# Two-layer attention and GLU kernel: second layer from its unit 3 on written in orders of four steps, with 16, 7 and 2 buffers of three kinds

## The chip, the cores and the metric

One core of a Trainium2 chip runs the whole program. The metric is the time of one execution on the device, in microseconds (us). Each kernel is run several times and the median is taken.

## The reference, cut to what matters

The same two sublayers run twice over 2048 rows of 448 numbers, in float32: attention with 16 query heads of 28 that share one key and one value head, then a gated unit of width 1792.

```python
def _A_ref(x, wq, wk, wv, wo):
    q = (x @ wq).reshape(B, S, H, Dh).transpose(0, 2, 1, 3)
    k = x @ wk
    v = x @ wv
    p = _softmax(jnp.einsum("bhqd,bkd->bhqk", q, k) * (Dh ** -0.5), axis=-1)
    o = jnp.einsum("bhqk,bkd->bhqd", p, v)
    return o.transpose(0, 2, 1, 3).reshape(B, S, H * Dh) @ wo

def _B_ref(x, w_gate, w_up, w_down):
    return (_sigmoid(x @ w_gate) * (x @ w_up)) @ w_down

x = A_x
x = x + _A_ref(_layernorm(x), wq, wk, wv, wo)
x = x + _B_ref(_layernorm(x), w_gate, w_up, w_down)
# and both once more, with the same weights
```

## The kernel before, in words

The 2048 rows are cut into 16 units of 128 query rows (`U`), the keys into 16 tiles of 128 (`KT`). A layer is a loop over 16 x 16 steps: in step `kt` of unit `u` the program makes the scores of the unit's 16 heads against one key tile. All instructions stand in the order in which the program writes them; each engine works through its own in that order.

Four kinds of work make up a step, and one letter stands for each in the strings of `PATHS`:

- **S** (`scores`, L580 to 588): one matmul of four heads (tile `s`, L584, 96 rows of keys by 512 columns), and on ScalarE the exponential of it into a tile `P` (L587). A step has four.
- **P** (`pv`, L590): the values. The four `P` tiles of one earlier step are multiplied with `VV`, each by a float32 matmul that uses 32 columns of the array (L595, at column positions 0, 32, 64 and 96), and summed over the unit's steps in one PSUM tile `pv`. In the trace each of these matmuls is two records, so one step's values are eight. Steps whose values are still to be made stand in the list `waiting`.
- **M** (`Maxima.step`): the row maxima of a later unit, which the scores need as an offset. Four matmuls `mx` use 32 rows of the array each (L549, at row positions 0, 32, 64 and 96) and fill four PSUM tiles; VectorE reduces each (L554, tile `mp`).
- **F** (`fill.slice`): a slice of everything else on the TensorE. The feed-forward of a block of two units (`TB` = 2) runs here: seven passes of `glu` with 44 matmuls for the gate (`gp`) and for the up projection (`up`, both L352), then the down projection (`dn`, L784), and the output projection of the attention (`wo`, L695). Each F gives out as many nanoseconds of it as `rate` says, so that what is left is spread over the steps that are left; 28 us of it (`KEEP`) stay for the end.

**X** issues the next stage of the chain that follows a unit's values (sums, division, output projection, layer norm) and has no time of its own on the TensorE.

A pair of strings describes two successive steps: the first one's order and the second's. "A" and "B0"/"B1" are the first layer's, "C" the second layer's units 0 to 2. From unit 3 on the second layer takes "D0" for even and "D1" for odd units. There the values of two steps are made together in the first of two steps, behind its four scores.

All PSUM tiles but `pv` share seven banks (`NBK`). A bank that was given back longest ago is taken next, so an S or an M waits until the exponential, the reduction or the GLU's activation that reads that bank's last contents is done. In SBUF, `P` has 12 buffers, the GLU's products `h` have 10 (`HB`), and the tag `s2` has three: it holds `th`, the gate's tanh (L746), which VectorE multiplies with `up` (L754) and from which the two halves of `h` are made (L757 on ScalarE, L758 on VectorE). At the start of the program the 16 tiles of the input take ten buffers of `h` and six of `P` (`load_x0`), and `s2` holds scratch of the scales (`junq`) and copies of query projections (`qf`, L409).

Of the kernel before, what the change touches and what calls it, by code (L numbers as in the profile page):

```python
# [8 lines left out]
F32 = mybir.dt.float32  # L9
# [10 lines left out]
def interleaved_layers_kernel(ctx: ExitStack, tc: tile.TileContext, x, wq, wk, wv, wo, wg, wu, wd, out, layers=2):  # L20
# [7 lines left out]
    _, S, D = x.shape  # L28
    F = wg.shape[1]
    H, Dh = 16, 28  # L30
    NT, NB, G, KT, FC = S // 128, S // 512, H // 4, S // 128, F // 128
    U = NT
    TB, WB, HB = 2, 4, 10
    NBL = NT // TB
    EPS = 1e-5

# [5 lines left out]
    wk1 = ctx.enter_context(tc.tile_pool(name="wk1", bufs=2))  # L42
# [37 lines left out]
    def fps(shape, dt, name):  # L80
        flush()
        return psf.tile(shape, dt, tag="f", name=name, bufs=NBK["f"])
# [262 lines left out]
    def chain(ps, W, X, cost, w_first):  # L345

        pairs = PAIRS if w_first else sorted(PAIRS, key=lambda a: a[2])
        for n, (part, c, xc, k) in enumerate(pairs):
            a, b = W(part, c, k), X(xc, k)
            if not w_first:  # L350
                a, b = b, a
            nc.tensor.matmul(ps, a, b, start=n == 0, stop=n == 10)  # L352
            yield cost
# [43 lines left out]
    def qproj(l, XT, b, g):  # L397
        p = fps([128, 512], F32, "qp")
        yield from chain(p, lambda a, c, k: WQ[:k, a, c, 4 * g:4 * g + 4].rearrange("p h d -> p (h d)"),
                         lambda c, k: XT[:k, c], C512, True)  # L400
        by_pool = early[0] or (l, b) == (1, 1)

        def ev():
            q = wk1.tile([128, 2, 512], F16, name="qst")
            hi = QH0[:, g] if l + b == 0 else q[:, 0]
            nc.scalar.activation(hi, p, AF.Copy, scale=2.0 ** -18)
            if by_pool:
                f = wk1.tile([128, 512], F32, tag="s2", name="qf", bufs=3)
                nc.scalar.activation(f, p, AF.Copy, scale=2.0 ** -18)  # L409

            def lo():
                QDONE[l, b] = QDONE.get((l, b), 0) + 1
                if by_pool:
                    nc.gpsimd.tensor_tensor(q[:, 1], f, hi, op=OP.subtract)
                else:
                    nc.vector.scalar_tensor_tensor(q[:, 1], p, 2.0 ** -18, hi, op0=OP.mult, op1=OP.subtract)
                if l + b == 0:
                    nc.sync.dma_start(qd[0][0, g, 0], hi)
                    nc.sync.dma_start(qd[0][0, g, 1], q[:, 1])
                else:  # L420
                    nc.gpsimd.dma_start(qd[l % 2][b, g].rearrange("l p n -> p l n"), q)
            defer(lo)
        defer(ev)
# [157 lines left out]
    def scores(l, u, kt, g, P):  # L581
        assert ("m", l, u) in stored, (l, u, kt)
        s = psf.tile([128, 512], F32, tag=BANKS["s"], name="s", bufs=NBK[BANKS["s"]])
        nc.tensor.matmul(s, KK[l][0:96, 0, kt * 128:(kt + 1) * 128], QS[l, u][:, g].rearrange("p h n -> p (h n)"),  # L584
                         start=True, stop=True)
        p = wk1.tile([128, 512], F32, tag="P", name="P", bufs=12)
        nc.scalar.activation(p, s, AF.Exp, scale=esc)  # L587
        P.append(p)

# [32 lines left out]
    class Block:  # L622
# [109 lines left out]
        def bulk(self):  # L732
            l, b, XT2 = self.l, self.b, self.XT2
            hs = []

            def glu(f):

                for j in range(2):
                    if f + j + 2 < FC:
                        self.load_w(f + j + 2)  # L740
                w = [self.wt.pop(f + j) for j in range(2)]
                gp = fps([128, 2, TB * 128], F32, "gp")
                for j in range(2):
                    yield from chain(gp[:, j], lambda a, c, k: w[j][:k, 0, a, c], lambda c, k: XT2[:k, c], C256, True)
                th = wk1.tile([128, 512], F32, tag="s2", name="th", bufs=3)
                defer(lambda: nc.scalar.activation(th, gp.rearrange("p j n -> p (j n)"), AF.Tanh, scale=gsc))  # L746
                up = fps([128, 2, TB * 128], F32, "up")
                for j in range(2):
                    yield from chain(up[:, j], lambda a, c, k: w[j][:k, 1, a, c], lambda c, k: XT2[:k, c], C256, True)
                h = wk1.tile([128, 2, 512], F16, name="h", bufs=HB)  # L750

                def ev():
                    t = th
                    nc.vector.scalar_tensor_tensor(t, th, 1.0, up.rearrange("p j n -> p (j n)"), op0=OP.add, op1=OP.mult)  # L754

                    def parts():
                        nc.scalar.activation(h[:, 0], t, AF.Copy, scale=2.0 ** -17)  # L757
                        defer(lambda: nc.vector.scalar_tensor_tensor(h[:, 1], t, 2.0 ** -17, h[:, 0], op0=OP.mult,  # L758
                                                                     op1=OP.subtract), 3)
                    defer(parts, 3)  # L760
                defer(ev)
                hs.append(h)

            for f in range(0, FC, 2):
                yield from glu(f)

            if not self.last and b % 2 == 0:
                XTQ[l + 1, b // 2] = big.tile([128, 7, 512], F16, tag="big", name="XT1")
            need(2 + FC)
            for t in range(TB):  # L770
                yield from self.down(t, hs)
# [113 lines left out]
    fill = Filler()  # L885
# [7 lines left out]
    xr0 = {}  # L893

    def load_x0(i, eng=nc.sync):
        if i < HB:
            xr0[i] = wk1.tile([128, D], F32, tag="h", name="xr0", bufs=HB)
        else:
            xr0[i] = wk1.tile([128, D], F32, tag="P", name="xr0", bufs=12)
        eng.dma_start(xr0[i], x[0, i * 128:(i + 1) * 128])  # L900

    hl0, ls0 = {}, {}
# [77 lines left out]
    nmx = 0  # L980

    def qsq(c):
        junk = wk1.tile([128, D], F32, tag="s2", name="junq", bufs=3)
        squares(parts[:, c:c + 1], rq[:, c], junk)

    def qsum():
# [45 lines left out]
    for b in range(1, NB):  # L1032
# [5 lines left out]
    HEAD = U * KT - 32  # L1038
    sparse = ()
    PATHS = {  # L1040
        "A": ("FFSFSSFSPXM", "FSFSFSSPXM"),
        "B0": ("FSFSSXSPPM", "SFFSSFFXMFS"),
        "B1": ("FSFSFXSFSPMP", "SSFSFFXSFM"),
        "C": ("FFSXSSSPPM", "SFFXFFSMSSF"),
        "D0": ("FFXFSSSSPPM", "FFSFSXSFFMS"),
        "D1": ("FSFXSFSSPPM", "SSFFFXSFSFM"),
    }

    def pair_of(l, u):
# [9 lines left out]
    for l in range(layers):  # L1059
# [20 lines left out]
        rate = 0.0  # L1080
        for step in range(U * KT):
            u, kt = divmod(step, KT)
            if step == HEAD and not final:
                mxs[l + 1] = Maxima(l + 1)
            P = []
            pair = pair_of(l, u)
            single = "P" in pair[0] and "P" in pair[1]
            for o in pair[kt % 2]:
                if o == "S":
                    scores(l, u, kt, len(P), P)  # L1090
                elif o == "M":
                    if l and step < 3 * KT:
                        n = step in sparse
                    else:
                        n = 1 + (u == 0 and kt in MORE)
                    if not n:
                        mx.visit()
                    for _ in range(n):
                        if not mx.step() and not final and l + 1 in mxs:
                            a = mxs[l + 1].between()  # L1100
                            if a and soon(a[0], mxs[l + 1].need(a)):
                                mxs[l + 1].step(a)
                    if kt == 2 and u + 1 < U:
                        load_qs(l, u + 1)
                elif o == "P":
                    for _ in range(len(waiting) if single else min(1, len(waiting))):
                        pv(*waiting.pop(0))
                elif o == "X":
                    if u and kt == 1:
                        b = (u - 1) // TB  # L1110
                        if (l, b) not in BLK:
                            BLK[l, b] = Block(l, b)
                        later(*BLK[l, b].tile(u - 1))
                    if l == 0:
                        paced(step)
                    tick()
                    fed = sum(BLK[l, b].fed == TB for b in range(NBL) if (l, b) in BLK)
                    if fed < NBL - 1:
                        rate = fill.left / max(FIRST + TB * KT * fed - step, 1)
                    else:  # L1120
                        rate = max(fill.left - KEEP, 0) / (U * KT - step)
                else:
                    fill.slice(2 * rate / "".join(pair).count("F"))
            waiting.append((l, u, kt, P))
        while waiting:
            pv(*waiting.pop(0))
# [46 lines left out]
```

## Time and profile before

| what | us |
|---|---|
| median of 3 runs | 2245.24 (2240.86 to 2248.77) |
| the profiled execution's own time | 2247.71 |
| span of the instructions in it | 2245.9 |
| second layer, unit 3's first score to unit 15's last (13 units) | 1350.5 to 2158.3: about 808 |
| an odd unit and the next even unit there | 62.6 and 63.35 |
| last score to end of the span | about 88 |

The profiled execution lies 2.5 us above the median of the runs, of which 1.8 us lie around the span. The shares of the span by engine are PE 98%, VectorE (DVE) 73%, ScalarE (ACT) 69%. In the timeline, start times on PE are recorded; how long a matmul took is modelled and includes its way through the array, so the distance from one start to the next is what a matmul costs in a stream.

### The profile page before, as it was taken

How to read it: one execution, taken by the hardware profiler on the slowest of the kernel's cores; microseconds unless marked ns; L12 is line 12 of the kernel's file. 1: busy time of each engine (PE TensorE's matmuls, PEld its weight loads, DVE VectorE, ACT ScalarE, POOL GpSimd, SP SyncE). 2: the span in 40 equal slices, each digit the busy share in tenths (PEclk: the TensorE clock that was granted, in tenths of full speed). 3: DMA queues.
4: the chain of work that ended last, by engine and by line, in shares of the span. 5: the costliest groups of instructions: out<-in, count | busy, mean ns of one | idle time of the engine just before them, and what ended most of it. 6: DMA issues, size and time to landing. Idle time of an engine off the chain costs nothing.

```text
span 2245.9 us, 41454 instructions
## 1 busy us (share of the span) xinstructions
PE 2195.5 (98%) x15915; PEld 1030.8 (46%) x15915; DVE 1643.7 (73%) x2905; ACT 1552.8 (69%) x2595; POOL 335.9 (15%) x590
## 2 busy tenths in 40 slices
PE   7998999999999999999999999999999999999999
PEld 3322344444544445454564324445454544445467
DVE  7888888777777787777796557777777777777222
ACT  5698777776667677676614997777676767777741
POOL 5113764101010100101012010000000000000010
PEclk9999999999999999999999999999999999999999
DMA  4333662323313232331441113323231313223233
GB/s 143 106 97 94 197 215 81 106 79 85 112 60 102 64 100 90 97 107 49 119 154 35 36 52 108 80 88 99 67 108 49 100 59 103 76 88 96 75 118 108
DMA packets 203622, 213.28 MB, mean 95 GB/s; under 512 B 135376, under 2 KB 164240, under 8 KB 203424
## 3 DMA queue, kind: packets, MB, share of 16 engines
q1 hardware_dynamic: 198080, 195.78, 29.2%
q0 software_dynamic: 5344, 14.87, 1.9%
q8 instruction: 124, 2.03, 0.4%
q14 instruction: 74, 0.61, 0.1%
HBM read 175.37 MB, written 23.59 MB: 89 GB/s over the span
## 4 chain that ended last, share of the span: by engine, by line
PE 86%; DVE 8%; ACT 2%; issue 1%; DMA 1%; SPq 1%; POOL 0%; DVEq 0%; ACTq 0%; POOLq 0%
PE pv L595 20%; PE s L584 19%; PE up L352 11%; PE dn L784 11%; PE gp L352 11%; PE mx L549 7%; DVE mp L554 6%; PE wo L695 3%; PE qp L352 2%; ACT P L587 1%; DMA wgu<-wgu_d 0%; DMA rq<-in_A_wq_dram 0%; DMA rc<-sums 0%; PE hot L916 0%; DVE sgu L131 0%
## 5 line engine op out<-in xcount | busy, mean ns | idle before, releaser
L587 ACT ACTIVATE P<-s,esc 128x512 f32<-128x512 f32 x2048 | 1297.8, 690 | 474.5 <-PE s L584 462.8
L554 DVE TENSOR_REDUCE mp<-mx 128x1 f32<-128x512 f32 x2048 | 1269.4, 682 | 389.2 <-PE mx L549 385.4
L584 PE MATMUL s<-QS,KK 96*128 96x512 f16 x2048 | 673.8, 381 | 21.3 <-DVE mp L554 14.8
L352 PEld LDWEIGHTS <-wgu 128*128 128x128 f16 x4928 | 467.6, 97 | 182.1 <-issue 42.9
L595 PE MATMUL pv<-P,VV 128*32 128x512 f32 x4096 | 510.7, 602 | 0.0
L352 PE MATMUL gp<-XT,wgu 128*128 128x256 f16 x2464 | 349.2, 272 | 2.4 <-DVE mp L554 1.7
L352 PE MATMUL up<-XT,wgu 128*128 128x256 f16 x2464 | 348.3, 272 | 0.7 <-DVE mp L554 0.7
L784 PE MATMUL dn<-WD,h 128*128 128x448 f16 x1344 | 301.0, 352 | 0.0
L584 PEld LDWEIGHTS <-KK 96*128 96x128 f16 x2048 | 189.7, 97 | 212.5 <-issue 114.5
L595 PEld LDWEIGHTS pv<-P,VV 128*32 128x32 f32 x4096 | 98.7, 108 | 244.6 <-issue 242.6
L549 PE MATMUL mx<-KK,QH 32*128 32x512 f16 x1792 | 185.3, 386 | 3.0 <-DVE mp L554 1.7
L784 PEld LDWEIGHTS <-h 128*128 128x128 f16 x1344 | 126.5, 97 | 129.4 <-issue 14.5
L549 PEld LDWEIGHTS <-QH 32*128 32x128 f16 x1792 | 46.0, 91 | 256.5 <-issue 252.7
L669 POOL TENSOR_TENSOR lb<-pvs,lb 128x512 f32<-128x512 f32 x32 | 41.1, 1284 | 739.1 <-DMA lb<-sums 619.8
L757 ACT ACTIVATE h<-th 128x512 f16<-128x512 f32 x112 | 70.3, 628 | 61.8 <-DVE th L754 61.5
L754 DVE SCALAR_TENSOR_TENSOR th<-th,up 128x512 f32<-128x512 f32 x112 | 76.2, 680 | 48.9 <-PE up L352 42.2
L306 POOL TENSOR_SCALAR rs<-mv 128x1 f32<-128x1 f32 (+1 forms) x50 | 11.2, 225 | 656.6 <-DVE mv L291 573.6
L352 PE MATMUL qp<-XT,WQ 128*128 128x512 f16 x352 | 108.3, 390 | 0.7 <-DVE mp L554 0.4
L746 ACT ACTIVATE th<-gp,gsc 128x512 f32<-128x512 f32 x112 | 76.8, 685 | 32.8 <-PE gp L352 32.6
L758 DVE SCALAR_TENSOR_TENSOR h<-th,h 128x512 f16<-128x512 f32 x112 | 79.9, 713 | 20.8 <-ACT h L757 20.8
L695 PE MATMUL wo<-WO,oT 128*128 128x448 f16 x384 | 89.7, 352 | 0.2 <-ACT P L587 0.2
L352 PEld LDWEIGHTS <-WQ 128*128 128x128 f16 x352 | 32.9, 99 | 54.9 <-issue 28.9
(151 smaller groups left out, 918.1 us busy)
## 6 DMA issues: line engine op xcount, KB each, us to landing
wgu<-wgu_d SPq DMA_DIRECT2D x224, 512.0 KB
QS<-qd SPq DMA_DIRECT2D x384, 32.0 KB
lb<-sums SPq DMA_DIRECT2D x128, 64.0 KB
xr<-in_A_x_dram SPq DMA_DIRECT2D x32, 224.0 KB
qd<-qst POOLq DMA_DIRECT2D x28, 256.0 KB, 2.7
wgu_d<-sgu POOLq DMA_DIRECT2D x14, 512.0 KB, 3.7
x2d<-x SPq DMA_DIRECT2D x16, 224.0 KB
xr<-x2d SPq DMA_DIRECT2D x16, 224.0 KB
```

The costliest lines, as they stand in the source:

```text
L352: nc.tensor.matmul(ps, a, b, start=n == 0, stop=n == 10)
L549: nc.tensor.matmul(ps[h][:, i * w:(i + 1) * w], qh[32 * h:32 * h + 32, g], KK[l][32 * h:32 * h + 32, 1, ka:kz], start=True, stop=True, til ...
L554: nc.vector.tensor_reduce(o, ps[h].rearrange("p (g k) -> p g k", g=n), axis=AX.X, op=OP.max)
L584: nc.tensor.matmul(s, KK[l][0:96, 0, kt * 128:(kt + 1) * 128], QS[l, u][:, g].rearrange("p h n -> p (h n)"), start=True, stop=True)
L587: nc.scalar.activation(p, s, AF.Exp, scale=esc)
L595: nc.tensor.matmul(v[32 * g:32 * g + 32], VV[l][:, kt], P[g], start=kt == 0, stop=kt == KT - 1, tile_position=(0, 32 * g))
L695: nc.tensor.matmul(p, v["oT"][:, a, h * 128:(h + 1) * 128], WO[:, c, h], start=n == 0, stop=n == 11)
L746: defer(lambda: nc.scalar.activation(th, gp.rearrange("p j n -> p (j n)"), AF.Tanh, scale=gsc))
L754: nc.vector.scalar_tensor_tensor(t, th, 1.0, up.rearrange("p j n -> p (j n)"), op0=OP.add, op1=OP.mult)
L757: nc.scalar.activation(h[:, 0], t, AF.Copy, scale=2.0 ** -17)
L758: defer(lambda: nc.vector.scalar_tensor_tensor(h[:, 1], t, 2.0 ** -17, h[:, 0], op0=OP.mult, op1=OP.subtract), 3)
L784: nc.tensor.matmul(p, hs[f // 2][:, a, o:o + 128], WD[:, f, c], start=n == 0, stop=n == 3 * FC - 1)
```

## The change

The strings of "D0" and "D1" become four each: the order is now written for four steps, and which string a step takes is `kt % 4`. The letters of four steps are the same in number (16 S, 4 M, 4 X, 4 P; D1 has 15 F in place of 16, and each gives out correspondingly more). The values (P) stand at the end of the first step and in the second: one step's at the end of the first, the others before and after the maxima of the second. In the third and the fourth step there are none. Since up to 16 probability tiles now wait for their values, `P` has 16 buffers; `h` has 7 and `s2` has 2. At the start the input therefore takes seven buffers of `h` and nine of `P`.

```diff
-    TB, WB, HB = 2, 4, 10
+    TB, WB, HB = 2, 4, 7
...
-                f = wk1.tile([128, 512], F32, tag="s2", name="qf", bufs=3)
+                f = wk1.tile([128, 512], F32, tag="s2", name="qf", bufs=2)
...
-        p = wk1.tile([128, 512], F32, tag="P", name="P", bufs=12)
+        p = wk1.tile([128, 512], F32, tag="P", name="P", bufs=16)
...
-                th = wk1.tile([128, 512], F32, tag="s2", name="th", bufs=3)
+                th = wk1.tile([128, 512], F32, tag="s2", name="th", bufs=2)
...
-        "D0": ("FFXFSSSSPPM", "FFSFSXSFFMS"),
-        "D1": ("FSFXSFSSPPM", "SSFFFXSFSFM"),
+        "D0": ('FFXFSSSSP', 'MPPFSXSPMFFFSS', 'XSFFFSFSMFSFF', 'SSXFSFMS'),
+        "D1": ('FFXFSSSSP', 'PMPSFFXSPMFSFS', 'FSFSSFXMFSF', 'SFSFSFXMS'),
...
-            single = "P" in pair[0] and "P" in pair[1]
-            for o in pair[kt % 2]:
+            single = len(pair) == 2 and "P" in pair[0] and "P" in pair[1]
+            for o in pair[kt % len(pair)]:
...
-                    fill.slice(2 * rate / "".join(pair).count("F"))
+                    fill.slice(len(pair) * rate / "".join(pair).count("F"))
```

The tiles `xr0` and `junq` take the same new numbers of buffers. "A" to "C" keep their orders.

On PE, in an even unit (unit 8 of the second layer, first step of a group of four): before, the last score is followed by the values of two steps and the maxima. The names are `s` score, `pv` values, `mx` maxima's product, with `KK` the keys, `QH` the queries' high halves and `VV` the values.

```order
L584 MATMUL s<-QS,KK 128x512
L595 MATMUL pv<-P,VV 32x512 x8
L549 LDWEIGHTS QH
L549 MATMUL mx<-KK,QH 128x512
L549 LDWEIGHTS QH
L549 MATMUL mx<-KK,QH 128x512
L549 LDWEIGHTS QH
L549 MATMUL mx<-KK,QH 128x512
L549 LDWEIGHTS QH
L549 MATMUL mx<-KK,QH 128x512
L352 LDWEIGHTS wgu
```

After the change the same place on PE reads so:

```order
L584 MATMUL s<-QS,KK 128x512
L595 MATMUL pv<-P,VV 32x512 x4
L549 LDWEIGHTS QH
L549 MATMUL mx<-KK,QH 128x512
L549 LDWEIGHTS QH
L549 MATMUL mx<-KK,QH 128x512
L549 LDWEIGHTS QH
L549 MATMUL mx<-KK,QH 128x512
L549 LDWEIGHTS QH
L549 MATMUL mx<-KK,QH 128x512
L595 MATMUL pv<-P,VV 32x512 x8
L352 LDWEIGHTS wgu
```

The run of eight has become a run of four, the maxima, and a run of eight; a third run, of four, follows further down in the same step, where before the next run was two steps away. In the whole stretch from unit 3's first score to the end, PE's order has 105 uninterrupted runs of values before and 152 after, and 188 groups of maxima in both.

On VectorE, a stretch around units 7 and 8 of the second layer, before (`mp` the maxima's reductions, `th` and `h` the GLU's):

```order
L554 TENSOR_REDUCE mp<-mx 128x1 x4
L754 SCALAR_TENSOR_TENSOR th<-th,up 128x512
L554 TENSOR_REDUCE mp<-mx 128x1 x8
L758 SCALAR_TENSOR_TENSOR h<-th,h 128x512
L554 TENSOR_REDUCE mp<-mx 128x1 x4
L754 SCALAR_TENSOR_TENSOR th<-th,up 128x512
```

The same stretch after the change:

```order
L554 TENSOR_REDUCE mp<-mx 128x1 x4
L754 SCALAR_TENSOR_TENSOR th<-th,up 128x512
L554 TENSOR_REDUCE mp<-mx 128x1 x4
L758 SCALAR_TENSOR_TENSOR h<-th,h 128x512
L554 TENSOR_REDUCE mp<-mx 128x1 x8
L754 SCALAR_TENSOR_TENSOR th<-th,up 128x512
```

The operations are the same; the GLU's stand before or behind another group of maxima here and there.

More of the change, by code (lines that the diff above doesn't have):

```diff
@@ L898, in load_x0 @@
         else:
-            xr0[i] = wk1.tile([128, D], F32, tag="P", name="xr0", bufs=12)
+            xr0[i] = wk1.tile([128, D], F32, tag="P", name="xr0", bufs=16)
         eng.dma_start(xr0[i], x[0, i * 128:(i + 1) * 128])
@@ L982, in qsq @@
     def qsq(c):
-        junk = wk1.tile([128, D], F32, tag="s2", name="junq", bufs=3)
+        junk = wk1.tile([128, D], F32, tag="s2", name="junq", bufs=2)
         squares(parts[:, c:c + 1], rq[:, c], junk)
@@ L1040, in interleaved_layers_kernel @@
     PATHS = {
[L1041 to L1044, printed above, removed]
-        "D0": ("FFXFSSSSPPM", "FFSFSXSFFMS"),
-        "D1": ("FSFXSFSSPPM", "SSFFFXSFSFM"),
+        "A": ('FFSFSSFSPXM', 'FSFSFSSPXM'),
+        "B0": ('FSFSSXSPPM', 'SFFSSFFXMFS'),
+        "B1": ('FSFSFXSFSPMP', 'SSFSFFXSFM'),
+        "C": ('FFSXSSSPPM', 'SFFXFFSMSSF'),
+        "D0": ('FFXFSSSSP', 'MPPFSXSPMFFFSS', 'XSFFFSFSMFSFF', 'SSXFSFMS'),
+        "D1": ('FFXFSSSSP', 'PMPSFFXSPMFSFS', 'FSFSSFXMFSF', 'SFSFSFXMS'),
     }
```

## The prediction

> **What bounds the kernel now.** I read the page's busy shares first, then the stretch that the change touches (from 1350 us, the second layer's unit 3, to its last score at 2158 us) by the windows and by the chain that ended last, and then the timeline wherever the chain leaves PE. The page and the windows (each with span, then PE, PEld, DVE, ACT, POOL busy) say:
>
> ```profile
> PE 2195.5 (98%) x15915; PEld 1030.8 (46%) x15915; DVE 1643.7 (73%) x2905; ACT 1552.8 (69%) x2595; POOL 335.9 (15%) x590
> 1601.00:1727.00 126.00, 125.93 (x932) 60.55 (x931) 96.09 (x165) 90.53 (x146) 9.58 (x20) 1.00 0.28 83
> 2104.00:2158.00 54.00, 54.00 (x399) 28.98 (x398) 8.69 (x15) 43.38 (x72) 3.99 (x9) 1.00 0.34 107
> ```
>
> PE has work all the time at a granted clock of 1.00, and the others idle a quarter of it. The chain over that stretch of 808 us gives PE nearly everything, but not all:
>
> ```profile
> by line: PE pv L595 23.6%; PE s L584 23.1%; PE gp L352 14.1%; PE up L352 13.9%; PE dn L784 12.1%; PE mx L549 7.5%; PE wo L695 2.8%; DVE mp L554 1.5%; issue 0.6%; ACT P L587 0.4%; DVE th L754 0.1%; PE qp L352 0.1%; DVE xn L329 0.1%; PE mt L5
> ```
>
> VectorE's reductions, issue and the exponentials have 1.5 + 0.6 + 0.4 = 2.5%, 20 us. That is what an order with better places could win at most, if the chain's pieces were time in which PE stood. They are not. One piece comes back every 126 us; the chain has it so:
>
> ```profile
> 1639.39 0.13 DVE mp L554
> 1639.51 0.47 issue
> 1639.98 1.29 DVE mp L554 x2
> 1641.27 0.04 issue
> ```
>
> That is 1.93 us off PE. PE's own timeline over the same time:
>
> ```profile
> 1639.28 0.74 PE L695 MATMUL wo<-WO,oT 128*128 128x448 f16 x3
> 1639.86 0.38 PE L584 MATMUL s<-QS,KK 96*128 96x512 f16 x1
> 1640.08 0.73 PE L695 MATMUL wo<-WO,oT 128*128 128x448 f16 x3
> 1640.65 1.05 PE L584 MATMUL s<-QS,KK 96*128 96x512 f16 x3
> 1641.62 0.64 PE L595 MATMUL pv<-P,VV 128*32 128x512 f32 x4
> ```
>
> PE worked through most of it: only the three scores are late. From their start to the values lie 0.97 us; three scores take 0.74 (two at 0.22 and the last, ahead of values, 0.30; the rows for that come next). PE stood 0.23 us of the 1.93, an eighth. By that share the 20 us are 2.5 us of standing; for a few places that lose more I take 3 us. So this stretch is the sum of PE's starts, and the change is to be priced by what it does to them.
>
> **What a change of shape costs on PE.** An even unit's two steps before (start, modelled duration):
>
> ```profile
> 1687.39 1.03 PE L584 MATMUL s<-QS,KK 96*128 96x512 f16 x4
> 1688.35 1.92 PE L595 MATMUL pv<-P,VV 128*32 128x512 f32 x16
> 1690.20 0.39 PE L549 MATMUL mx<-KK,QH 32*128 32x512 f16 x4
> 1690.53 1.05 PE L352 MATMUL up<-XT,wgu 128*128 128x256 f16 x8
> 1692.51 0.93 PE L352 MATMUL up<-XT,wgu 128*128 128x256 f16 x7
> 1693.37 0.39 PE L549 MATMUL mx<-KK,QH 32*128 32x512 f16 x4
> 1693.69 0.39 PE L584 MATMUL s<-QS,KK 96*128 96x512 f16 x1
> ```
>
> Four scores take 0.96, of which the last has 0.30, since 3 x 0.22 go to the others: 0.09 are lost on entering the values. A run of two steps' values (16 records) takes 1.85. A group of maxima takes 0.33 ahead of anything. Seven `up` take 0.86 ahead of maxima, where 0.11 each would be 0.77: again 0.09. The first layer's odd units show what the new order has, a run of one step's values, maxima, and a run of one step's values:
>
> ```profile
> 565.53 1.07 PE L595 MATMUL pv<-P,VV 128*32 128x512 f32 x8
> 566.53 0.39 PE L549 MATMUL mx<-KK,QH 32*128 32x512 f16 x4
> 566.86 1.07 PE L595 MATMUL pv<-P,VV 128*32 128x512 f32 x8
> 567.85 0.60 PE L584 MATMUL s<-QS,KK 96*128 96x512 f16 x2
> ```
>
> A single run takes 1.00 ahead of maxima and 0.99 ahead of scores, so two cost 1.99 where one double run costs 1.85: **each run that is cut off costs 0.14 us**. The maxima between them cost the same 0.33 as ahead of scores; standing beside values saves them nothing.
>
> The Trainium skill, "TensorEngine Tiling (Array Packing)", section Key Properties, speaks against the change: a change of the tiling mode, other than a change of the tile alone, drains the TensorE. The rows agree in direction. "TensorE: Matmul & The Clock Gate", Step-by-step, puts the array's drain at about 128 cycles; at the 2.4 GHz that it gives, an estimate of 0.05 us each, by which the term that follows would be 47 x 0.05 = 2.5 us. The measured 0.14 decides.
>
> **The new orders.** Before, four steps have two runs of values (each of two steps) and four groups of maxima. Now even units have P, M, PP and later P, M; odd units PP, M, P and later P, M: three runs, and the same four groups. The built order confirms it for the whole stretch: 105 runs before, 152 after, 188 groups of maxima in both. The sum: 47 more runs x 0.14 = **+6.6 us**. The other matmuls are the same in number, and nothing on another engine can hide this, since PE is what all of it waits for.
>
> **The waits.** What the new orders can give back is the 3 us. VectorE's reductions and ScalarE's exponentials in the same two steps:
>
> ```profile
> 1690.62 2.48 DVE L554 TENSOR_REDUCE mp<-mx 128x1 f32<-128x512 f32 x4 [1.54 <-PE mx L549]
> 1693.79 2.48 DVE L554 TENSOR_REDUCE mp<-mx 128x1 f32<-128x512 f32 x4 [0.68 <-PE mx L549]
> 1687.96 2.41 ACT L587 ACTIVATE P<-s,esc 128x512 f32<-128x512 f32 x4
> 1691.83 1.92 ACT L587 ACTIVATE P<-s,esc 128x512 f32<-128x512 f32 x3 [1.46 <-PE s L584]
> ```
>
> Maxima now stand 3.17 and about 4.6 us apart, and VectorE needs 2.48 for a group. In the new orders I add up the letters from group to group. A step takes 126 / 32 = 3.94 us, of which scores have 0.88, values 0.97 and maxima 0.38, each with its entry; that leaves 1.71, or 0.43 for each of four F. Even units then have 4.0, 4.4, 3.3 and 3.7 us between groups, odd ones 3.7, 3.6, 3.4 and 4.9. All leave VectorE more than the shortest gap of before. So the reductions wait less often.
>
> ScalarE is the tighter one where GLU's tanh falls between two groups, because the third group of an odd unit takes banks that three exponentials and the tanh must free. I went through one such place in the built order by start distances. The group's fourth bank is freed by the fourth of a burst on ScalarE: two exponentials, the tanh, an exponential. The burst's first score starts 2.85 us ahead of the group's fourth matmul (a score, three `gp`, a score, three `gp`, an `up`, a score, four `up`, two scores, four `up`, by the distances above), and its exponential can begin 0.42 us later (0.38 of the matmul, 0.04 of issue): 2.43 us are left. A burst takes 0.69 for the first and 0.58 for each that follows (2.41 for four): 2.43, and 0.04 of issue, so the bank is some 0.05 us late; with 0.69 for each, 2.76 and 0.04, 0.3 us late or a little more. 47 groups of four steps with one such place each bound the new waits: 2.4 us and 14 us. The bursts are what the trace has in such places, so I stay near the low end: 3.5 us.
>
> **Buffers.** `s2` with two buffers: the third tanh waits for the first's last reader. The closest place in the trace that I found, at the turn of the layers:
>
> ```profile
> 1166.97 0.67 ACT L746 ACTIVATE th<-gp,gsc 128x512 f32<-128x512 f32 x1
> 1178.28 0.69 ACT L746 ACTIVATE th<-gp,gsc 128x512 f32<-128x512 f32 x1 [0.86 <-PE gp L352]
> 1175.47 0.68 DVE L758 SCALAR_TENSOR_TENSOR h<-th,h 128x512 f16<-128x512 f32 x1
> 42.17 2.27 POOL L414 TENSOR_TENSOR qst<-qf,QH 128x512 f16<-128x512 f32 x2
> 44.94 0.60 ACT L409 ACTIVATE qf<-qp 128x512 f32<-128x512 f32 x1
> ```
>
> The reader is done at 1176.15, 2.1 us ahead of the tanh after the next. In the prologue the fourth copy `qf` would wait for the second's reader, the first of the two on GpSimd, done at about 43.3, 1.6 us ahead of it. `h` with seven: a block makes seven, and its first is written after 44 matmuls of GLU (4.8 us) that follow the last block's down projection, which reads them. Both cost nothing; without that cover, a tanh that is late by 1 us once in each of the 16 blocks would cost 16 us. The 16 `P` are just what can be waiting (12 at a group's start and four new). The end stays PE's: after the last score only a run of values more (one step's, moved there) and three matmuls fewer stand.
>
> **The sum.** +6.6 (runs) - 3 (waits before) + 3.5 (waits after) = +7.1 us. The profiled execution took 2247.71; the median of the runs is 2245.24, and I put the difference on the median: **2252.3 us**. A measurement of this kernel can tell about 0.3%, 6.7 us, from no change, so my sum lies just beyond it.
>
> **Rivals.**
>
> - *No change that can be told (on the other side of my sum).* The mechanism is the evened distance of the maxima: with at least 3.3 us between groups against 2.48 of reduction, no matmul finds its bank taken, and the waits after the change are 0.5 us or less. The place is the score that takes the first bank behind a group. Then +6.6 - 3 + 0.5 = +4 us: 2249. It decides as soon as the new waits stay under 3.1 us, which is close to my 3.5. Against it speaks the tanh place; for it, that before has almost no waits with less room. 0.40.
> - *The tanh place is late by 0.3 us every time.* +6.6 - 3 + 14 = +17.6: 2263. For it: besides exponentials ScalarE has 9 tasks a unit (7 tanh and 7 `h` in two units, two copies in each), 2.25 per group of four steps, so such places are not rare. Against: ScalarE idles 1.46 us ahead of a burst above. 0.12.
> - *The chain is right after all*: all of its 20 us are time that PE lost, and the new order removes them: -20 + 6.6 = -13: 2232. Against it are PE's own starts. 0.08.
>
> **How the numbers follow.** My forecast has 0.40, and with the rival that is slower still, slower by over 0.3% has 0.52; within 0.3% has 0.40, faster 0.08. The range leaves out the gain and the upper part of the late tanh: 2247 to 2260.
>
> **What would show it.** In the new profile single runs of `pv` (x8) with 1.00 us to the next start, and 47 more of them; an odd and an even unit together about 1 us longer than 126; PE busy still all of each window. I am wrong if a cut-off run costs nothing there, if unit pairs get shorter, or if PE stands ahead of the third maxima's group for tenths of a microsecond each time.

## The result and the profile after

| | before | changed |
|---|---|---|
| median, us | 2244.85 (4 runs, 2240.86 to 2248.77) | 2256.54 (4 runs, 2254.94 to 2257.93) |
| ratio | | 1.0053 (95% interval 1.0040 to 1.0065) |
| span of the profiled execution | 2245.9 | 2255.8 |
| that execution's own time | 2247.71 | 2257.61 |
| first score of unit 3 to last score, second layer | 807.9 | 816.5 |
| last score to the end of the span | 87.6 | 88.9 |

The kernel became 0.53% slower, 9 to 15 us by the interval, 9.9 us by the spans. The stretch that the change touches has 8.6 of them. Nothing ahead of it moved: unit 3's first score comes at 1350.5 us in both traces. That they agree so closely is partly chance: in the traces of the other kernels below that have the same first layer, this point lies between 1346.4 and 1352.3 us. The stretch itself repeats much better, so it is the better measure.

The 1.8 us or so between a profiled execution's time and its span lie in every run, so they are no part of what sets the profiled run before above its median.

The page's busy shares, and a window over about an odd and the next even unit, as before (span, then busy time of PE, PEld, DVE, ACT, POOL, then granted clock, DMA share and GB/s):

```profile
PE 2206.6 (98%) x15915; PEld 1025.6 (45%) x15915; DVE 1643.5 (73%) x2905; ACT 1550.1 (69%) x2595; POOL 335.4 (15%) x590
1605.00:1733.00 128.00, 127.98 (x934) 59.83 (x932) 96.57 (x166) 89.83 (x146) 9.10 (x20) 1.00 0.27 82
```

PE is busy for all of the window at a granted clock of 1.00, the whole program has the same 15915 matmuls, and yet such a pair of units now takes 62.04 + 65.59 = 127.63 us in place of 125.95. A busy share cannot tell that. The chain over the stretch shows one thing more:

```profile
by line: PE pv L595 24.3%; PE s L584 23.1%; PE gp L352 14.2%; PE up L352 14.1%; PE dn L784 12.1%; PE mx L549 8.1%; PE wo L695 3.8%; PE qp L352 0.1%; ACT P L587 0.1%; issue 0.1%; ACT pvs L599 0.1%; PE mt L575 0.1%; ACT qst L406 0.0%
```

VectorE's 1.5% are gone from it, as the new places of the maxima promise, and the stretch is longer all the same. What the chain gave VectorE before was not time that PE lost. The timeline of PE has the loss; an even unit's first two steps of four:

```profile
1667.26 1.03 PE L584 MATMUL s<-QS,KK 96*128 96x512 f16 x4
1668.22 1.06 PE L595 MATMUL pv<-P,VV 128*32 128x512 f32 x8
1669.21 0.40 PE L549 MATMUL mx<-KK,QH 32*128 32x512 f16 x4
1669.54 1.92 PE L595 MATMUL pv<-P,VV 128*32 128x512 f32 x16
1671.40 0.61 PE L352 MATMUL up<-XT,wgu 128*128 128x256 f16 x4
1671.84 0.60 PE L584 MATMUL s<-QS,KK 96*128 96x512 f16 x2
1672.37 1.06 PE L595 MATMUL pv<-P,VV 128*32 128x512 f32 x8
1673.37 0.40 PE L549 MATMUL mx<-KK,QH 32*128 32x512 f16 x4
1673.70 1.37 PE L352 MATMUL up<-XT,wgu 128*128 128x256 f16 x11
```

From start to start, the single runs of values take 0.99 and 1.00 us and the double one 1.86: four steps' values cost 3.85 where two double runs cost 3.70. That is 0.15 for one run more, as the first layer's rows had it.

The rest is waiting. For every two neighbouring kinds of matmul there is a usual distance between their starts (the median; among values, at the same place in the run). Where a single distance is over 0.03 us longer, the excess is counted as a wait. These sum to 3.5 us in this stretch before and 6.9 after. Almost all of the 6.9, 6.0 us, is the fourth matmul of a group of maxima, which waits for its bank. The waits of before, mostly at scores behind scores or behind maxima, are gone; these are new. Two such places on PE, then the engines that release the banks:

```profile
1645.62 0.60 PE L584 MATMUL s<-QS,KK 96*128 96x512 f16 x2
1646.14 0.78 PE L549 MATMUL mx<-KK,QH 32*128 32x512 f16 x4
1646.86 0.39 PE L352 MATMUL up<-XT,wgu 128*128 128x256 f16 x2
...
1717.50 0.69 PE L549 MATMUL mx<-KK,QH 32*128 32x512 f16 x4
1718.12 1.92 PE L595 MATMUL pv<-P,VV 128*32 128x512 f32 x16
```

```profile
1645.82 0.68 DVE L691 SCALAR_TENSOR_TENSOR x<-wo,osc,xr 128x448 f32<-128x448 f32 x1 [0.56 <-PE wo L695]
...
1715.93 2.42 ACT L587 ACTIVATE P<-s,esc 128x512 f32<-128x512 f32 x4 [1.04 <-PE s L584]
```

A group that meets no wait shows 0.39 and is 0.33 ahead of what follows. The first here shows 0.78 and 0.72: its fourth matmul starts at 1646.56, when VectorE has read the output projection out of its bank (done at 1646.50). The second shows 0.69 and 0.62: it stands behind a single run, and the third of the four exponentials, done at about 1717.78, frees its last bank.

### The profile page after: what moved, and what is told of

It reads as the page before. It is cut to its first block, busy times and chain, and to the rows that moved or that the text cites. A ratio compares the mean times of both kernels' runs of the same rounds, so it can differ in the third digit from the quotient of the medians.

```text
span 2255.8 us, 41436 instructions
## 1 busy us (share of the span) xinstructions
PE 2206.6 (98%) x15915; PEld 1025.6 (45%) x15915; DVE 1643.5 (73%) x2905; ACT 1550.1 (69%) x2595; POOL 335.4 (15%) x590
## 4 chain that ended last, share of the span: by engine, by line
PE 86%; DVE 8%; ACT 2%; DMA 2%; issue 1%; POOL 0%; SPq 0%; DVEq 0%; ACTq 0%; POOLq 0%
PE pv L595 20%; PE s L584 19%; PE dn L784 11%; PE up L352 11%; PE gp L352 11%; PE mx L549 7%; DVE mp L554 6%; PE wo L695 3%; PE qp L352 2%; ACT P L587 1%; DMA rd<-in_B_w_down_dram 1%; DVE sgu L131 0%; DMA rc<-sums 0%; DMA rq<-in_A_wq_dram 0%; PE hot L916 0%
## 5 line engine op out<-in xcount | busy, mean ns | idle before, releaser
L595 PE MATMUL pv<-P,VV 128*32 128x512 f32 x4096 | 519.5, 602 | 0.4 <-ACT pvs L599 0.4
L352 PE MATMUL up<-XT,wgu 128*128 128x256 f16 x2464 | 354.9, 272 | 0.7 <-DVE mp L554 0.7
L584 PEld LDWEIGHTS <-KK 96*128 96x128 f16 x2048 | 194.4, 97 | 224.4 <-issue 123.2
L595 PEld LDWEIGHTS pv<-P,VV 128*32 128x32 f32 x4096 | 94.0, 108 | 225.1 <-issue 218.0
L549 PE MATMUL mx<-KK,QH 32*128 32x512 f16 x1792 | 190.7, 385 | 3.1 <-DVE mp L554 1.8
```

The source lines that it names most:

```text
L549: nc.tensor.matmul(ps[h][:, i * w:(i + 1) * w], qh[32 * h:32 * h + 32, g], KK[l][32 * h:32 * h + 32, 1, ka:kz], start=True, stop=True, til ...
L595: nc.tensor.matmul(v[32 * g:32 * g + 32], VV[l][:, kt], P[g], start=kt == 0, stop=kt == KT - 1, tile_position=(0, 32 * g))
```

## The experiments

The theory: each cut-off run of values costs 0.14 us of PE, and waits for banks come on top. The rivals: that runs are free and the loss is waits or the late values; that the smaller buffers cost. "Runs" below are the uninterrupted runs of `pv` on PE from unit 3's first score on, "waits" the sum just described over the same stretch.

**The buffers alone.** The kernel before, with 16 `P`, 7 `h`, 2 of `s2`:

```diff
-    TB, WB, HB = 2, 4, 10
+    TB, WB, HB = 2, 4, 7
```

(and the other five numbers of the change's diff)

> The kernel before with the new numbers of buffers alone (16 P, 7 h, 2 of s2), old orders. Theory (cut-off runs of values cost, buffers nothing): 0 us against before, within 2 us, and no tanh or h product that waits for a buffer. Rival (fewer h and s2 buffers cost): +5 to +11 us, most of what the whole change cost.

2245.88 against 2245.53 us; ratio 0.9997 (0.9988 to 1.0006), waits 3.4 us. The medians and the ratio fall on the two sides of no change, both inside the scatter, and the trace's stretch takes 807.84 us where it took 807.86. The buffers cost nothing and give nothing.

**All runs cut, in the kernel before.** Two-step orders, 12 `P`:

```diff
-        "D0": ("FFXFSSSSPPM", "FFSFSXSFFMS"),
-        "D1": ("FSFXSFSSPPM", "SSFFFXSFSFM"),
+        "D0": ("FFXFSSSSPMP", "FFSFSXSFFMS"),
+        "D1": ("FSFXSFSSPMP", "SSFFFXSFSFM"),
```

> The kernel before with its orders of two steps and all its buffers, but the maxima set between the two steps' values (PMP in place of PPM): 200 runs in the stretch in place of 105. Theory: 95 x 0.14 = +13 us against before, and single runs of 8 records that take 1.00 us to the next start. Rival (cutting a run is free; the time is in lag, buffers and waits for the tanh): +0 to +3 us.

2260.51 against 2245.53 us, ratio 1.0066 (1.0053 to 1.0078): +15 us with 95 runs more. Its PE timeline:

```profile
1613.53 0.60 PE L584 MATMUL s<-QS,KK 96*128 96x512 f16 x2
1614.05 1.06 PE L595 MATMUL pv<-P,VV 128*32 128x512 f32 x8
1615.05 0.39 PE L549 MATMUL mx<-KK,QH 32*128 32x512 f16 x4
1615.38 1.07 PE L595 MATMUL pv<-P,VV 128*32 128x512 f32 x8
1616.37 0.60 PE L584 MATMUL s<-QS,KK 96*128 96x512 f16 x2
```

Single runs take 1.00 and 0.99 here too; 95 x 0.14 = 13.3 us, and the waits rose from 3.5 to 6.1. Both together are 15.9. No late value, no third or fourth string and no other buffer is in this kernel, so the 0.14 us belong to the cut, and the rise of the waits comes with it.

**Odd units alone cut**, as many runs as the changed kernel has:

```diff
-        "D1": ("FSFXSFSSPPM", "SSFFFXSFSFM"),
+        "D1": ("FSFXSFSSPMP", "SSFFFXSFSFM"),
```

> The kernel before with the runs of values cut by the maxima in odd units alone (PMP in place of PPM): 153 runs in the stretch, as many as the changed kernel has, without its lag of the values, its order of four steps and its buffers. Theory: 48 x 0.14 = 6.7 us and half the waits of the kernel with all runs cut, 1.5 us: +8 us against before. Rival (a cut costs only by the waits that it makes): under +3 us.

2253.67 against 2246.26 us, ratio 1.0034 (1.0023 to 1.0046): +7.4 us, with waits of 4.9. By the sum, 48 x 0.14 + 1.4 = 8.1.

**Two runs in four steps.** The changed kernel with the maxima behind the first run:

```diff
-        "D0": ('FFXFSSSSP', 'MPPFSXSPMFFFSS', 'XSFFFSFSMFSFF', 'SSXFSFMS'),
-        "D1": ('FFXFSSSSP', 'PMPSFFXSPMFSFS', 'FSFSSFXMFSF', 'SFSFSFXMS'),
+        "D0": ('FFXFSSSSP', 'PPMFSXSFFPMFSS', 'XSFFFSFSMFSFF', 'SSXFSFMS'),
+        "D1": ('FFXFSSSSP', 'PPMSFFXSFPMSFS', 'FSFSSFXMFSF', 'SFSFSFXMS'),
```

> The changed kernel, but in the second step the maxima stand behind the values of the first run, so that four steps have two runs of values again (104 in the stretch in place of 152); the values still stand in the first two of four steps, with 16 P buffers. Theory (runs cost 0.14 us each): 48 x 0.14 = 6.7 us less than the changed kernel, so +2 to +6 us against before, the rest being waits. Rival (the long lag of the values and bank waits cost, runs nothing): as slow as the changed kernel, +10 to +12 us.

2257.91 against 2245.53 us, ratio 1.0055 (1.0041 to 1.0068): as slow as the changed kernel, as the rival had it, but not for its reason, that runs cost nothing. The trace shows that both terms are there and cancel. A run of three steps' values and a single one:

```profile
1608.03 2.78 PE L595 MATMUL pv<-P,VV 128*32 128x512 f32 x24
1610.75 0.39 PE L549 MATMUL mx<-KK,QH 32*128 32x512 f16 x4
...
1612.89 1.06 PE L595 MATMUL pv<-P,VV 128*32 128x512 f32 x8
1613.89 0.39 PE L549 MATMUL mx<-KK,QH 32*128 32x512 f16 x4
```

2.72 and 1.00 us, 3.72 for four steps: the 0.14 per run are saved. But the waits went up to 14.7 us, 11 more than before: here the maxima follow each other after 3.14 us, with other work on VectorE between them, which is the likely reason and was not tried by itself. Of the 14.7 us, 5.0 are within groups of maxima and most of the others at scores.

**One run in four steps**, one order for all units:

```diff
+        "D0": ('FFXFSSSSP', 'PPPMFSXFSFFSFMS', 'FSFXSFSFMFS', 'FSXFSFSFMS'),
```

(and the same for "D1")

> The changed kernel with both orders replaced by one in which the values of four steps are a single run behind the scores of the first (53 runs in the stretch), maxima behind them and at three later places about 3.0 to 3.4 us apart. Theory: 52 runs fewer than before, 52 x 0.14 = -7 us, and 57 changes of shape that go with them are in that price or add up to 0.1 us each at the places where a whole visit falls away (5 us more); with 3 us of waits -5 to -9 us against before. Rival (waits and the lag of the values cost, runs nothing): +3 us or more.

2277.30 against 2245.53 us, ratio 1.0144 (1.0128 to 1.0161). With 52 runs fewer the waits are 41 us, of which 11.7 are one place in each unit:

```profile
1673.41 2.78 PE L595 MATMUL pv<-P,VV 128*32 128x512 f32 x24
1676.90 1.07 PE L595 MATMUL pv<-P,VV 128*32 128x512 f32 x8 [0.70 <-ACT pvs L599]
```

The run goes over a unit's end, and the next unit's values must wait until ScalarE has copied `pv` out of its only bank.

**One run at the start of four steps**, so that no run goes over a unit's end:

```diff
+        "D0": ('PPPPMFSFSXFSFSF', 'FMFSFSXFSFSF', 'FMFSFSXFSFS', 'FXFMSSSS'),
```

(and the same for "D1")

> The changed kernel with one order for all units from 3 on: the values of the four steps before in one run at the very start of the first step, maxima behind them and three more groups 3.6 us apart, the fourth step's scores last. 52 runs in the stretch in place of 105, 443 changes of shape in place of 503; no run crosses a unit's end. Theory: 53 x 0.14 = -7 us against before if the waits stay near before's 3.5 us; each unit's copy of pv is no longer waited for. Rival (orders of four steps and late values cost by themselves): slower than before, +5 us or more.

2308.43 against 2246.26 us, ratio 1.0279 (1.0265 to 1.0293). The copy of `pv` is no longer waited for; the waits are 73 us, 48 of them scores behind scores:

```profile
1715.06 0.39 PE L549 MATMUL mx<-KK,QH 32*128 32x512 f16 x4
1715.38 0.60 PE L584 MATMUL s<-QS,KK 96*128 96x512 f16 x2
1716.22 0.38 PE L584 MATMUL s<-QS,KK 96*128 96x512 f16 x1 [0.24 <-DVE mp L554]
1716.82 0.38 PE L584 MATMUL s<-QS,KK 96*128 96x512 f16 x1 [0.22 <-DVE mp L554]
```

Two scores find free banks behind a group of maxima, the third and the fourth wait for reductions. The next run takes these four scores apart, to tell the fault of this order from that of long runs.

**The same with the scores spread:**

```diff
+        "D0": ('PPPPMFSFXSFSFS', 'FSMFSFXSFS', 'FSFSMFXSFS', 'FSFSFMFXSS'),
```

(and the same for "D1")

> As the kernel with one run of values at the start of every four steps, but with two scores in place of four behind the fourth group of maxima, and the others spread singly between F, so that no third score follows a group before its first bank is reduced. In the run before it the scores that stand behind the fourth group waited 0.24 and 0.22 us each time. Theory: those waits go, 52 runs stay 53 fewer than before: -7 us against before with waits of 3.5 us, 0 us with waits of 10. Rival (a run of 3.6 us leaves too little room between the other groups for VectorE, wherever the scores stand): +10 us or more.

2272.21 against 2244.87 us, ratio 1.0116 (1.0098 to 1.0134): the rival's side. Waits are down to 36 us and sit at the fourth matmul of the maxima (15.8) and at scores. While a run of 3.6 us goes on, no maxima are made; the other three groups and the scores share what is left, and the waits take more than four times what the runs save. An order in which a run of four pays was not found, and that none exists is not shown.

**The third group of maxima later.** The changed kernel:

```diff
-        "D1": ('FFXFSSSSP', 'PMPSFFXSPMFSFS', 'FSFSSFXMFSF', 'SFSFSFXMS'),
+        "D1": ('FFXFSSSSP', 'PMPSFFXSPMFSFS', 'FSFSSFXFMSF', 'SFSFSFXSM'),
```

> The changed kernel; in odd units the third group of maxima stands one F later and the fourth one S later. In the trace of after the third group's fourth matmul is late there by 0.40, 0.12 and 0.05 us in each pair of units, waiting for a bank that ScalarE or VectorE still reads. Theory (runs 6.6 us, waits the rest): those 0.57 us of each pair go, 6 pairs, 3 us less than the changed kernel; about +8 us against before. Rival (waits are most of the loss): 6 us less or more. If the shorter way to the fourth group makes new waits: no change against the changed kernel.

2260.88 against 2246.26 us, ratio 1.0064 (1.0052 to 1.0077): not faster than the changed kernel, but slower by 3 us between the medians. Their intervals against before overlap; the traces are clearer: from unit 3's first score to the end it takes 5.1 us more, of which 4.7 are waits, which rose from 6.9 to 11.6 us. Those at the fourth matmul stayed in sum (6.0 to 6.8), and scores now wait as well. Moving two groups made new late places, and no run here has the changed kernel's runs without its waits.

**Runs joined in the first layer.** The kernel before, second layer untouched:

```diff
-        "B1": ("FSFSFXSFSPMP", "SSFSFFXSFM"),
+        "B1": ("FSFSFXSFSPPM", "SSFSFFXSFM"),
```

> The kernel before, second layer as it was; in the first layer's odd units from 5 on the single run, maxima, single run (PMP) become one run and the maxima behind it (PPM): 48 runs fewer. Theory: 48 x 0.14 = -6.7 us against before, less what new waits cost: -2 to -6 us. Rival (the price of a cut run holds only in the second layer's orders): 0 us.

2252.06 against 2246.26 us, ratio 1.0023 (1.0014 to 1.0032): 5.8 us slower, against both forecasts. PE at the place that the prediction quotes from the first layer:

```profile
564.63 1.92 PE L595 MATMUL pv<-P,VV 128*32 128x512 f32 x16
566.49 0.40 PE L549 MATMUL mx<-KK,QH 32*128 32x512 f16 x4
566.81 0.39 PE L584 MATMUL s<-QS,KK 96*128 96x512 f16 x1
567.65 0.38 PE L584 MATMUL s<-QS,KK 96*128 96x512 f16 x1 [0.45 <-DVE mp L554]
```

Runs and maxima take 1.86 + 0.32 us where they took 2.32 before: 0.14 are saved. But the second score stands 0.62 us too late, since VectorE began with the maxima a run later. From unit 4's first score to the first layer's last score the waits rose from 8.3 to 21.9 us: -48 x 0.14 + 13.6 = +6.9, and that stretch grew from 780.16 to 787.02 us, by 6.9. So a run is cut there for a reason: the cut's 0.14 lets VectorE begin 0.86 us earlier.

The runs that change the second layer's orders or buffers beside each other. The sum is 0.14 us for each run more, plus the rise of the waits. "In the traces" is the difference from unit 3's first score to the end of the span, which leaves out the scatter ahead of it:

| kernel | runs | waits, us | sum, us | in the traces, us | between the medians, us |
|---|---|---|---|---|---|
| before | 105 | 3.5 | | | |
| buffers alone | 105 | 3.4 | -0.1 | -0.2 | +0.4 |
| changed kernel | 152 | 6.9 | +10.0 | +9.9 | +11.7 |
| odd units cut | 153 | 4.9 | +8.1 | +8.5 | +7.4 |
| all units cut | 200 | 6.1 | +15.9 | +15.9 | +15.0 |
| third group later | 152 | 11.6 | +14.7 | +15.0 | +14.6 |
| two runs in four steps | 104 | 14.7 | +11.1 | +11.6 | +12.4 |
| one run, spread | 52 | 36.2 | +25.3 | +24.8 | +27.3 |
| one run | 53 | 41.0 | +30.2 | +29.9 | +31.8 |
| one run first | 52 | 72.6 | +61.7 | +61.2 | +62.2 |

Two terms give every difference in the traces within about 0.5 us and every difference of the medians within 2 us, over differences from 0 to 62. The waits are read from the same traces, so this is a balance and not a forecast: it shows that no third term, such as a cost of late values by themselves, is needed. What causes a wait is shown only at the places quoted.

## Why the prediction was right, and where its size was off

- **PE's starts bound the stretch, and the chain's 20 us were not there to win**: right. They left the chain, and the stretch grew by 8.6 us.
- **47 runs more at 0.14 us, +6.6 us**: right. The rows after have 3.85 us in place of 3.70 for four steps, and the cut kernels have the same price without the rest of the change. (The sign "47 more" holds for all runs; single runs, x8, went from none to 99, since a double run is cut into two single ones.) The Trainium skill ("TensorEngine Tiling (Array Packing)", Key Properties) says that a change of the tiling mode drains the TensorE, and the 0.14 us agree with it in direction. The prediction's estimate of 2.5 us, from the 128 cycles that the Trainium skill ("TensorE: Matmul & The Clock Gate", Step-by-step) gives for the drain, would have been too low by more than half.
- **Waits of 3 us before**: 3.5 by the starts.
- **New waits of 3.5 us**: this is the term that was mis-sized. It is 6.9 us. The place worked through in the prediction, the third group of an odd unit behind the tanh, exists:

```profile
1629.69 0.60 PE L584 MATMUL s<-QS,KK 96*128 96x512 f16 x2
1630.13 0.60 PE L352 MATMUL up<-XT,wgu 128*128 128x256 f16 x4
1630.66 0.49 PE L549 MATMUL mx<-KK,QH 32*128 32x512 f16 x4
1631.09 0.61 PE L352 MATMUL up<-XT,wgu 128*128 128x256 f16 x4
```

  Its group takes 0.43 to the next start in place of 0.32, 0.11 us late, where 0.05 was taken. But the prediction took one such place in each of the 47 groups of four steps. Only 24 of them are in odd units, and a third group is late by about this much once in a pair of units, five times or 0.6 us in all. In a pair there are six late places, between 0.05 and 0.40 us, and the two largest are others: a third group of an odd unit that needs the output projection's bank (0.40), and the group behind a single run that needs the third exponential (0.31). They are found only by following each bank through the order. That 3.5 came within a factor of two of 6.9 is therefore luck; that waits move to the fourth matmul of the maxima was right. One sign of being wrong came in part: PE stands 0.40 us within a third group, but once in an odd unit and not each time.
- **Buffers at nothing**: right, by the run with them alone.
- **The end**: the last score to the end took 1.3 us more. The prediction had a run of one step's values moved there (0.86 us inside a run, 1.00 alone) and three matmuls fewer (0.33 us); what is moved into the end is missing in the stretch, and the sum gives it no term. The rest is within the scatter: kernels whose end has the same matmuls as before took 87.4 to 88.2 us for it.
- **The rivals**: the one with hardly any waits fell because the waits went up and not down. The one with 14 us of waits had twice the size, and its tanh place is late by 0.11 us and not by 0.3. That the chain's 20 us were real fell with the first point.

With the right size of that term the sum is +6.6 - 3.5 + 6.9 = +10.0 us, against 9.9 in the traces and 11.7 between the medians; the remaining 1.7 us are within the scatter of the runs before (8 us).

## What to carry to other kernels

Where the tensor engine is full, read its start-to-start distances and not its busy share or the chain's shares: price each change of tile shape by them, and count in the built order how many a new order adds. Cutting a run of one shape can still pay, where it lets another engine begin earlier and a wait of that engine is larger than the cut: here 0.14 us against 0.62 in the first layer, and against next to nothing in the second (3.5 us of waits in 808). So tell the two terms apart, stream and waits, before moving either.

## What was not expected of the hardware

- Joining runs never won here, though each run saved its 0.14 us: with 52 runs fewer the streams of matmuls were 7 us shorter, and the waits for PSUM banks grew by 33 to 69 us. The order of before has 3.5 us of waits in 808 us with VectorE busy 76% of the time (96.09 of 126 us); by the balance above, another order with as many runs could win no more than these 3.5 us of waits there.
- A transposition `mt` behind a run of values costs no loss on entry, unlike the scores or maxima there: in the trace after, values to `mt` lie as far apart as two values in a run do, 0.41 us from the last record, while scores, maxima and `up` come after 0.525 us. In its rows `mt` uses 16 columns of the array (128*16) and the values 32 (128*32); whether that sets it apart was not tried.
